# First batch of a fused attention, MLP and expert kernel: another order of its head pairs, 128-wide transposes for two of them, and two units moved to a later place

## The chip, the cores and the metric

One core of one Trainium2 chip runs the whole program. The time is device microseconds (us) of one execution. The kernel before has a median of 770.23 us over three runs (769.16 to 770.8).

## What is computed

Three layers follow each other: masked attention over 4 batches and 8 heads, a gelu-like MLP over the 2304 rows that the attention gives, and an expert layer in which each row may go to one of 8 experts. Heads 0 to 3 use a local mask, heads 4 to 7 a strided one.

```python
    # attention: q, k, v are (4, 8, 576, 64)
    scores = scale * np.matmul(q, k.transpose(0, 1, 3, 2))
    mask_local = (rel >= 0) & (rel < stride)                    # stride = 32
    mask_strided = (rel >= 0) & (pos[None, :] % stride == pos[:, None] % stride)
    attn = np.exp(scores - max); attn = attn / (sum + 1e-09)
    return np.matmul(attn, v)
    # MLP: x is (2304, 512), w_in (512, 2048), w_out (2048, 512)
    h = x @ w_in
    g = h * (1.0 / (1.0 + np.exp(-1.702 * h)))
    return g @ w_out
    # experts: rows with x @ w_skip > 0 get x + gate * (relu(x @ w1[e]) @ w2[e]), e = argmax of x @ w_gate
```

## The kernel before

The 8 heads are worked on as four pairs, called hp: hp 0 and 1 are local, hp 2 and 3 strided. A pair is first loaded (`load_qk`), then transposed by TensorE into `qT` and `kb` (`emit_T`, with the copies out of PSUM in `t_evac`), then worked through in three units of up to two windows each (u = 0, 1, 2). A unit has three parts: S1 multiplies q by k into `sc`, adds the mask (VectorE, "pt,st<-sc,mloc" or "mstr"), takes the exponential (ScalarE) and normalises (GpSimd); S2 transposes the probabilities (`tp`, `pT`); S3 multiplies by V (`pv`) and writes the result as a high and a low part into `xT`, the input of the MLP. The rows of the strided V are first permuted through a DRAM buffer `vp_d` by transfers of GpSimd's queue (`permute_v`), and then loaded into `vstr`.

The MLP runs in 9 groups of 256 rows with 16 steps each. Step m of a group is `emit_A` (12 matmuls into `h` with the weights wi[m], then ScalarE's tanh and VectorE's product "g<-g,h") and, two steps later, `emit_B` (6 matmuls into `acc` with wo[m]). The weights come as fp32 and are split into a high and a low part before use, 32 tiles of 128x1024 in all. One such conversion (`conv_w`, "conversion" below) is three VectorE operations through a PSUM tile (L169, L170, L171), one ScalarE copy (L175) and one GpSimd subtraction (L176). Step m needs 2m conversions. The first group of the MLP is written behind batch 0's attention, and batch 1's attention runs between the first group's steps.

Each engine takes its instructions in one fixed order. The kernel writes its pieces in program order (`attn_pieces(0)`, from piece CV0 on a conversion after every third one, then the steps), and a scheduler that models the engines' times may move instructions of different engines and pieces against each other. SP issues nearly all loads, in order as well: an issue that has to wait holds up those behind it. Batch 0's order of pairs is 0, 2, 1, 3. The numbers in names such as raw_114 or p_165 tell buffers apart.

Of the kernel before, what the change touches and what calls it, by code (L numbers as in the profile page):

```python
# [31 lines left out]
FBT = 1  # L32
# [16 lines left out]
AS, AE = 3, 2  # L49
CV0, CV1 = 16, 3  # L50
WN = [0, 0, 2, 4]
PM, PC = 10, 15
# [6 lines left out]
AS1 = 9  # L59
KD = (0, 2)  # L60


@with_exitstack
def attn_moe_moe_kernel(ctx: ExitStack, tc: tile.TileContext, q, k, v, w_in, w_out, w_skip, w_gate, w1, w2, out):
# [11 lines left out]
    def big_tile(dt, name):  # L76
        return big.tile([128, 1024], dt, tag="big", name=name)
# [144 lines left out]
    with ExitStack() as ph1:  # L222
# [37 lines left out]
        def order(b):  # L260
            return [(b, 0), (b, 2), (b, 1), (b, 3)]

        def load_qk(b, hp):
            h0 = 2 * hp
            first = False
            if b == 0:
                raw = big_tile(F32, "raw0").rearrange("p (i h j d) -> p i h j d", i=2, j=4, h=2)
                if "tails" not in raws:
                    t = big_tile(F32, "tails")
                    raws["tails"] = t[:, 0 : H * D].rearrange("p (h d) -> p h d", h=H)  # L270
                    lst0.append(t[:, H * D : H * D + 256])
                    first = True
                rawt = raws["tails"][:, h0 : h0 + 2, :]
            else:
                raw = ap_.tile([128, 2, 4, 2, D], F32, tag="raw", bufs=2, name="raw")
                rawt = ap_.tile([128, 2, D], F32, tag="rawt", bufs=2, name="rawt")
            raws[b, hp] = raw, rawt
            for i, src in enumerate((q, k)):
                for h in range(2):
                    nc.sync.dma_start(out=raw[:, i, :, h, :] if b else raw[:, i, h, :, :], in_=src[b, h0 + h, 0:512, :].rearrange("(p j) d -> p j d", j=4))  # L280
                if b > 0:
                    nc.sync.dma_start(out=rawt[64 * i : 64 * i + 64], in_=src[b, h0 : h0 + 2, 512:576, :].rearrange("h p d -> p h d"))
            if first:
                for i, src in enumerate((q, k)):
                    nc.sync.dma_start(out=raws["tails"][64 * i : 64 * i + 64], in_=src[b, :, 512:576, :].rearrange("h p d -> p h d"))
# [38 lines left out]
        def t_evac(b, hp, jobs):  # L324
# [4 lines left out]
            for which, j, p in jobs:  # L329
                for lo, hi in ((0, 128),) if which == 0 else ((0, 64), (64, 128)):  # L330
                    d = [t_views(hp, qt[y] if which == 0 else kt[y][lo:hi, lo // 64], j) for y in ((z,) if b <= FB else (0, 1))]
                    ops.append((t_source(hp, p[lo:hi], j), d))
                    if b == 0 and hp in KD and which == 1:
                        nc.vector.tensor_copy(d[0], ops[-1][0])
# [12 lines left out]
        def emit_T(b, hp, which):  # L347
# [6 lines left out]
            for j in range(4):  # L354
                if b:
                    nc.tensor.transpose(out=p1[:, j, :], in_=raw[:, which, j].rearrange("p h d -> p (h d)"), identity=ident)  # L356
# [13 lines left out]
        def geom(hp, u, j):  # L370
# [8 lines left out]
            return w * RG * NTS, n, w * RG * NTS, n, mstr[0:n, 0:n]  # L379

        def ntile(hp, u):
            return 1 if hp >= 2 and u == 2 else 2

        def emit_S1(b, hp, u):
            nj = ntile(hp, u)
            sc = ps.tile([128, 2, 2, 128], F32, tag="sc" if b else ("sc", "acc0", "acc0")[u], name="sc")
            qn0 = geom(hp, u, 0)[1]
            for j in range(nj):
                q0, qn, k0, kn, _ = geom(hp, u, j)
                qt, kt = qk_bufs["q"], qk_bufs["k"]  # L390
                z = order(0).index((0, hp)) % 2
                prods = ((z, z),) if b <= FB else ((0, 0), (0, 1), (1, 0))
# [54 lines left out]
        def emit_S3(b, hp, u):  # L447
            pT = ust.pop((b, hp, u))
            nj = ntile(hp, u)
            qn = geom(hp, u, 0)[1]  # L450
            pv = ps.tile([128, 2 * 126], F32, tag="pv" if b else "acc1", name="pv")
            for j in range(nj):
# [49 lines left out]
        def attn_pieces(b):  # L502

            pairs = order(b)
            units = [(bb, hp, u) for bb, hp in pairs for u in range(3)]
            res = []
# [10 lines left out]
            for n in range(len(units) + 2):  # L517
                if n < len(units):
                    bb, hp, u = units[n]
                    if u == 0 and (b > FBT or n == 0):  # L520
                        res += T(n // 3)
                    res.append(lambda a=units[n]: emit_S1(*a))
                    if u == (TU1 if b else TU) and b <= FBT and n // 3 < 3:
                        res += T(n // 3 + 1)
                if 1 <= n <= len(units):
                    res.append(lambda a=units[n - 1]: emit_S2(*a))
                if n >= 2:
                    res.append(lambda a=units[n - 2]: emit_S3(*a))
                if n % 3 == 1 and n < len(units):
                    nx = pairs[n // 3 + 1] if n // 3 + 1 < 4 else order(b + 1)[0] if b + 1 < B else None  # L530
                    if nx and nx not in vt and (b or nx[0] == 0):
                        res.append(lambda a=nx: load_v(*a))
            return res


# [246 lines left out]
        nw = 0  # L782
        for n_, a in enumerate(order(0)):
            load_next_qk()
            if n_ == 0:
                permute_v(0, nc.gpsimd)
            load_v(*a)
            nw += WN[n_]
            loads_to(nw)
        for n_, p in enumerate(attn_pieces(0)):  # L790
# [4 lines left out]
        rq = []  # L795
        att = []
        nB = 0
        for s_ in range(NG * NM + LAG8):
            gi, m = divmod(s_, NM)
            if gi < NG:  # L800
# [22 lines left out]
                emit_A(gi, m)  # L823
            left_slots = 2 * (32 - (AE if s_ >= 32 else AE1) - s_ % 32)
            if att and s_ < NM:

# [265 lines left out]
```

## Time and profile before

| | |
|---|---|
| median of three runs | 770.23 us (769.16 to 770.8) |
| the profiled execution: its time, its span | 770.98 us, 769.3 us |
| TensorE matmul busy | 727.2 us (95% of the span) |
| VectorE, ScalarE, GpSimd busy | 357.1, 339.2, 164.0 us |
| TensorE's granted clock, 40 slices, tenths | 9985899999999999999999999999999899999998 |

The span is what lies between the first and the last instruction; some 1.7 us of the profiled execution's time lie around it. The profiled execution is 0.75 us above the median. Granted clock 1.00 is 2.4 GHz, 0.50 is 1.2 GHz. A slice of the last row is 19.2 us. In the rows further down, a busy time is that of an engine's instructions; "[idle before <-X]" is how long the engine had nothing to do ahead of a row and what released it.

### The profile page before, as it was taken

How to read it: one execution, taken by the hardware profiler on the slowest of the kernel's cores; microseconds unless marked ns; L12 is line 12 of the kernel's file. 1: busy time of each engine (PE TensorE's matmuls, PEld its weight loads, DVE VectorE, ACT ScalarE, POOL GpSimd, SP SyncE). 2: the span in 40 equal slices, each digit the busy share in tenths (PEclk: the TensorE clock that was granted, in tenths of full speed). 3: DMA queues.
4: the chain of work that ended last, by engine and by line, in shares of the span. 5: the costliest groups of instructions: out<-in, count | busy, mean ns of one | idle time of the engine just before them, and what ended most of it. 6: DMA issues, size and time to landing. Idle time of an engine off the chain costs nothing.

```text
span 769.3 us, 14169 instructions
## 1 busy us (share of the span) xinstructions
PE 727.2 (95%) x4977; PEld 636.6 (83%) x4977; DVE 357.1 (46%) x1452; ACT 339.2 (44%) x1096; POOL 164.0 (21%) x226
## 2 busy tenths in 40 slices
PE   7867999999999999999999999999999699999993
PEld 3545898788788888888888878988998699999993
DVE  2589886545456546355565534353452111121111
ACT  2695677565466566356665533342442111111110
POOL 4265665223013011202210202002021100000001
PEclk9985899999999999999999999999999899999998
DMA  8989811320302222221110010100683499981001
GB/s 244 354 282 258 269 32 34 80 47 11 103 5 66 61 53 39 68 59 22 43 46 1 10 37 15 33 25 14 195 153 99 127 395 397 353 261 41 16 13 33
DMA packets 95984, 84.44 MB, mean 110 GB/s; under 512 B 59412, under 2 KB 74964, under 8 KB 95904
## 3 DMA queue, kind: packets, MB, share of 16 engines
q1 hardware_dynamic: 92608, 78.39, 34.4%
q0 software_dynamic: 3296, 5.05, 2.0%
q8 instruction: 41, 0.67, 0.5%
q14 instruction: 39, 0.32, 0.3%
HBM read 71.00 MB, written 17.68 MB: 115 GB/s over the span
## 4 chain that ended last, share of the span: by engine, by line
PE 71%; issue 13%; DMA 10%; ACT 2%; DVE 2%; SPq 1%; POOL 0%; POOLq 0%; DVEq 0%; ACTq 0%
PE h L548 27%; PE acc L575 27%; DMA wx<-in_moe_w_dram 6%; PE sc L394 4%; PE pv L456 3%; PE tp L437 2%; PE p L360 2%; DMA out_dram<-res,xr 2%; PE p L356 1%; DMA raw<-in_q_dram 1%; PE tr L605 1%; PE p L359 1%; PE lc L619 1%; DMA tab_d<-rows,ix 1%; ACT kb L336 1%
## 5 line engine op out<-in xcount | busy, mean ns | idle before, releaser
L548 PE MATMUL h<-xT,wsp 128*128 128x256 f32 x1728 | 249.7, 289 | 1.3 <-ACT xT L472 1.3
L548 PEld LDWEIGHTS h<-xT,wsp 128*128 128x128 f32 x1728 | 232.1, 192 | 16.6 <-ACT xT L472 2.4
L575 PE MATMUL acc<-wsp,ghl 128*128 128x512 f32 x816 | 226.9, 403 | 0.5 <-ACT wsp L175 0.5
L575 PEld LDWEIGHTS acc<-wsp,ghl 128*128 128x128 f32 x816 | 141.3, 188 | 25.6 <-issue 2.0
L422 POOL TENSOR_TENSOR pt<-pt,st 96x256 f32<-96x256 f32 (+3 forms) x88 | 50.3, 589 | 258.3 <-DVE st L419 106.2
L552 DVE SCALAR_TENSOR_TENSOR g<-g,h 128x256 f32<-128x256 f32 x144 | 60.2, 419 | 92.6 <-ACT g L551 88.6
L551 ACT ACTIVATE g<-h 128x256 f32<-128x256 f32 x144 | 54.8, 382 | 101.6 <-PE h L548 91.9
L564 ACT ACTIVATE ghl<-g 128x256 fp32r<-128x256 f32 (+1 forms) x144 | 57.9, 404 | 59.5 <-DVE g L552 55.4
L932 PE MATMUL h<-xs,wx 128*128 128x160 f32 x512 | 77.7, 306 | 0.0
L412 ACT ACTIVATE pt<-pt,st 96x128 f32<-96x128 f32 (+3 forms) x176 | 67.3, 385 | 16.4 <-DVE st L404 16.0
L932 PEld LDWEIGHTS h<-xs,wx 128*128 128x128 f32 x512 | 73.0, 195 | 0.0
L933 ACT ACTIVATE hT<-h 128x160 f32<-128x160 f32 x64 | 19.4, 303 | 121.3 <-PE h L932 115.2
L941 PE MATMUL h<-hT,wx 128*128 128x160 f32 x512 | 72.4, 299 | 0.0
L565 DVE TENSOR_TENSOR ghl<-g,ghl 128x256 fp32r<-128x256 f32 (+1 forms) x128 | 53.6, 419 | 37.2 <-ACT ghl L564 29.5
L941 PEld LDWEIGHTS h<-hT,wx 128*128 128x128 f32 x512 | 70.3, 190 | 0.0
L394 PE MATMUL sc<-kb,qT 128*96 128x256 f32 (+3 forms) x220 | 45.6, 331 | 5.3 <-ACT kb L336 2.3
L696 POOL DMA_INDIRECT xs_d<-rows,ix x18 | 18.1, 1005 | 134.5 <-DVE ghl L565 36.9
L176 POOL TENSOR_TENSOR wsp<-wcv,wsp 128x512 fp32r<-128x512 f32 x32 | 41.1, 1284 | 22.2 <-ACT wsp L175 17.5
L956 POOL DMA_INDIRECT out_dram<-res,xr x16 | 14.6, 914 | 146.0 <-DVE res L953 87.1
L944 DVE COPY yT<-h 128x160 f32<-128x160 f32 x32 | 10.4, 325 | 75.7 <-PE h L941 75.7
L336 ACT ACTIVATE kb<-p 64x64 fp32r<-64x64 f32 (+3 forms) x56 | 38.5, 687 | 10.1 <-PE p L356 4.0
L394 PEld LDWEIGHTS sc<-kb,qT 128*96 128x96 f32 (+2 forms) x220 | 31.7, 176 | 11.6 <-issue 2.9
(151 smaller groups left out, 781.4 us busy)
## 6 DMA issues: line engine op xcount, KB each, us to landing
wx<-in_moe_w_dram SPq DMA_DIRECT2D x64, 512.0 KB
wraw<-in_moe_w_in_dram SPq DMA_DIRECT2D x16, 512.0 KB
wraw<-in_moe_w_out_dram SPq DMA_DIRECT2D x16, 512.0 KB
raw<-in_q_dram SPq DMA_DIRECT2D x32, 128.0 KB
raw<-in_k_dram SPq DMA_DIRECT2D x32, 128.0 KB
out_dram<-rows SPq DMA_DIRECT2D x16, 256.0 KB
xs_d<-zinit SPq DMA_DIRECT2D x1, 2570.0 KB
xr<-xs_d SPq DMA_DIRECT2D x16, 160.6 KB
```

The lines of the kernel that those rows point to most:

```text
L336: nc.scalar.activation(out=d[0], in_=ops[-1][0], func=AF.Copy)
L394: nc.tensor.matmul(out=sc[0:qn, j, :, 0:kn], lhsT=qt[a][:, q0 : q0 + qn], rhs=kt[c][:, :, k0 : k0 + kn], start=(n_ == 0), stop=(n_ == len( ...
L412: nc.scalar.activation(out=P[0:qn, j, h, 0:kn], in_=P[0:qn, j, h, 0:kn], func=AF.Exp, scale=-1.0, bias=st[0:qn, 0, i : i + 1], accum_out=s ...
L422: nc.gpsimd.tensor_tensor(out=P[0:qn, j, :, 0:kn], in0=P[0:qn, j, :, 0:kn], in1=st[0:qn, 1, 2 * j : 2 * j + 2, None].to_broadcast([qn, 2, ...
L548: nc.tensor.matmul(out=hp_, lhsT=wi[m][:, a, c, :], rhs=x[z], start=(n_ == 0), stop=(n_ == 3 * NC - 1))
L551: nc.scalar.activation(out=g, in_=hp_, func=AF.Tanh, scale=0.851)
L552: nc.vector.scalar_tensor_tensor(out=g, in0=g, scalar=1.0, in1=hp_, op0=ALU.add, op1=ALU.mult)
L564: nc.scalar.activation(out=t[:, 0], in_=g[:, a:z], func=AF.Copy)
L565: (nc.gpsimd if gi == 0 else nc.vector).tensor_tensor(out=t[:, 1], in0=g[:, a:z], in1=t[:, 0].bitcast(F32), op=ALU.subtract)
L575: nc.tensor.matmul(out=acc[gi, i], lhsT=ghl[i][:, a, :], rhs=wo[m][:, z, :], start=(m == 0 and n_ == 0), stop=(m == NM - 1 and n_ == 2),)
L932: nc.tensor.matmul(out=p, lhsT=wx[e, 0, c][:, 128 * m : 128 * m + 128], rhs=x, start=(c == 0), stop=(c == NC - 1))
L941: nc.tensor.matmul(out=p, lhsT=wx[e, 1, k_ // 2][:, o : o + 128], rhs=hT[e][k_ // 4][:, k_ % 4], start=(k_ == 0), stop=(k_ == NF - 1))
```

## The change

Batch 0's pairs go in the order 2, 3, 0, 1, so that the strided ones come first. Pairs 2 and 3 (those not in HM) are loaded with the two heads of a row beside each other, in pieces of 256 bytes rather than 1 KB, and transposed both heads at once, 128 wide. The third unit of pairs 0 and 1 is taken out of `attn_pieces(0)` and written between the first group's steps (`late_pieces`), with PSUM tiles of other tags. Conversions begin after piece 12 rather than 16 of a list that is now two units shorter. The loads of V and of the first weights are written in another order. KD and the condition behind it say which kb copies VectorE does in place of ScalarE: all of pairs 0 and 2 before, the lower half of pair 2 and all of pair 3 now.

```diff
-CV0, CV1 = 16, 3
-WN = [0, 0, 2, 4]
+CV0, CV1 = 12, 3
-KD = (0, 2)
+KD = (2, 3)
+HM = (0, 1)
         def order(b):
-            return [(b, 0), (b, 2), (b, 1), (b, 3)]
+            return [(b, hp) for hp in ((2, 3, 0, 1) if b == 0 else (0, 2, 1, 3))]
...
-                    nc.sync.dma_start(out=raw[:, i, :, h, :] if b else raw[:, i, h, :, :], in_=src[b, h0 + h, 0:512, :].rearrange("(p j) d -> p j d", j=4))
+                    nc.sync.dma_start(out=raw[:, i, h, :, :] if b == 0 and hp in HM else raw[:, i, :, h, :], in_=src[b, h0 + h, 0:512, :].rearrange("(p j) d -> p j d", j=4))
...
-                    if b == 0 and hp in KD and which == 1:
+                    if b == 0 and hp in KD and which == 1 and (lo == 0 or hp == 3):
                         nc.vector.tensor_copy(d[0], ops[-1][0])
...
             for j in range(4):
-                if b:
+                if b or hp not in HM:
                     nc.tensor.transpose(out=p1[:, j, :], in_=raw[:, which, j].rearrange("p h d -> p (h d)"), identity=ident)
...
+        def late_unit(b, hp, u):
+
+            return b == 0 and hp < 2 and u == 2
...
-            sc = ps.tile([128, 2, 2, 128], F32, tag="sc" if b else ("sc", "acc0", "acc0")[u], name="sc")
+            sc = ps.tile([128, 2, 2, 128], F32, tag="sc" if b or late_unit(b, hp, u) else ("sc", "acc0", "acc0")[u], name="sc")
...
-            pv = ps.tile([128, 2 * 126], F32, tag="pv" if b else "acc1", name="pv")
+            if late_unit(b, hp, u):
+                pv = ps.tile([128, 2 * 126], F32, tag="t", bufs=2, name="pv")
+            else:
+                pv = ps.tile([128, 2 * 126], F32, tag="pv" if b else "acc1", name="pv")
...
+        def late_pieces():
+            us = [(0, hp, 2) for hp in (0, 1)]
+            return [lambda f=f, a=a: f(*a) for f in (emit_S1, emit_S2, emit_S3) for a in us]
...
-        for n_, a in enumerate(order(0)):
-            load_next_qk()
-            if n_ == 0:
-                permute_v(0, nc.gpsimd)
-            load_v(*a)
-            nw += WN[n_]
-            loads_to(nw)
+        load_next_qk()
+        permute_v(0, nc.gpsimd)
+        load_next_qk()
+        load_next_qk()
+        load_v(0, 2)
+        load_v(0, 3)
+        loads_to(2)
+        load_next_qk()
+        load_v(0, 0)
+        load_v(0, 1)
+        nw = 4
+        loads_to(nw)
...
+            for _ in range(2):
+                if late_att:
+                    late_att.pop(0)()
```

What this does to TensorE's order shows at the very start of the program. These are its rows at the end of the first pair's transposes, before; p_165 and p_175 are that pair's q and k, each as eight pieces of 64 rows, and p_210 is the second pair's q:

```order
L359 MATMUL p_175<-ident,raw_114 64x128
L360 MATMUL p_175<-ident,raw_114 64x128
L344 MATMUL p_186<-ident,tails 128x128
L394 MATMUL sc<-kb,qT 96x2x96
L394 MATMUL sc<-kb,qT 96x256 x3
L359 MATMUL p_210<-ident,raw_129 64x128
L360 MATMUL p_210<-ident,raw_129 64x128
```

And these are TensorE's first rows now, where p_161 and p_167 are the first pair's q and k, p_198 and p_206 the second's:

```order
L357 MATMUL p_161<-ident,raw_114 128x128 x4
L357 MATMUL p_167<-ident,raw_114 128x128 x4
L345 MATMUL p_174<-ident,tails 128x128
L399 MATMUL sc<-kb,qT 126x2x126 x4
L357 MATMUL p_198<-ident,raw_126 128x128 x4
L357 MATMUL p_206<-ident,raw_126 128x128 x4
L399 MATMUL sc<-kb,qT 72x2x72
L442 MATMUL tp<-ident,pt 126x126 x2
```

Sixteen pieces of a pair have become eight, for the first two pairs; pairs 0 and 1 still have sixteen each.

The second place is VectorE's order around the first product of the MLP ("g<-g,h"). Before, its rows are:

```order
L170 SCALAR_TENSOR_TENSOR cvp<-wraw,cvp 128x512
L171 SCALAR_TENSOR_TENSOR wcv<-wraw,cvp 128x512
L492 TENSOR_TENSOR xT<-pv,xT 128x8x4 x2
L169 TENSOR_SCALAR cvp<-wraw 128x512
L170 SCALAR_TENSOR_TENSOR cvp<-wraw,cvp 128x512
L171 SCALAR_TENSOR_TENSOR wcv<-wraw,cvp 128x512
L169 TENSOR_SCALAR cvp<-wraw 128x512
L552 SCALAR_TENSOR_TENSOR g<-g,h 128x256 x2
L170 SCALAR_TENSOR_TENSOR cvp<-wraw,cvp 128x512
```

Now they are:

```order
L500 TENSOR_TENSOR xT<-pv,xT 128x128
L171 SCALAR_TENSOR_TENSOR wcv<-wraw,cvp 128x512
L500 TENSOR_TENSOR xT<-pv,xT 128x64
L500 TENSOR_TENSOR xT<-pv,xT 128x128
L169 TENSOR_SCALAR cvp<-wraw 128x512
L500 TENSOR_TENSOR xT<-pv,xT 128x128
L170 SCALAR_TENSOR_TENSOR cvp<-wraw,cvp 128x512
L171 SCALAR_TENSOR_TENSOR wcv<-wraw,cvp 128x512
L565 SCALAR_TENSOR_TENSOR g<-g,h 128x256
L169 TENSOR_SCALAR cvp<-wraw 128x512
L170 SCALAR_TENSOR_TENSOR cvp<-wraw,cvp 128x512
L565 SCALAR_TENSOR_TENSOR g<-g,h 128x256
```

Counted from the start of VectorE's order, 15 1/3 conversions stand ahead of the first product before, and 12 now; all of batch 0's attention, the two moved units too, still stands ahead of it.

The third place is TensorE's order where the MLP begins. Before, with v_141 and v_154 the V of pairs 1 and 3, and p_1084 and p_1093 the first transposes of batch 1:

```order
L548 MATMUL h<-xT,wsp 128x256 x2
L437 MATMUL tp<-ident,pt 72x72 x2
L548 MATMUL h<-xT,wsp 128x256 x4
L456 MATMUL pv<-pT,v_141 64x96 x4
L456 MATMUL pv<-pT,v_154 64x126 x4
L356 MATMUL p_1084<-ident,raw 128x128 x4
L456 MATMUL pv<-pT,v_154 64x126 x4
L456 MATMUL pv<-pT,v_154 64x72 x2
L548 MATMUL h<-xT,wsp 128x256 x2
L344 MATMUL p_1089<-ident,rawt 128x128
L356 MATMUL p_1093<-ident,raw 128x128 x4
L548 MATMUL h<-xT,wsp 128x256 x4
```

Now, with vloc and v_153 the V of pairs 0 and 1:

```order
L464 MATMUL pv<-pT,vloc 64x96 x4
L561 MATMUL h<-xT,wsp 128x256 x2
L442 MATMUL tp<-ident,pt 128x96 x4
L561 MATMUL h<-xT,wsp 128x256 x10
L464 MATMUL pv<-pT,v_153 64x96 x4
L464 MATMUL pv<-pT,vloc 64x96 x4
L464 MATMUL pv<-pT,v_153 64x96 x8
L561 MATMUL h<-xT,wsp 128x256 x12
L357 MATMUL p_1068<-ident,raw 128x128 x4
L561 MATMUL h<-xT,wsp 128x256 x12
L588 MATMUL acc<-wsp,ghl 128x512 x4
```

Before, the first two steps' matmuls are strewn among the attention of batch 0; now a step's twelve stand nearly together behind it. The second group begins as the first ends; from shortly ahead of the first run of 15 `acc` matmuls on (it stands between the first two transposes "tr<-ident,rows"), TensorE's order is the same in both kernels to the program's end, apart from line numbers, and so are the orders of the other engines from about there.

## Rows read from the trace of the kernel before

**Rows 1.** Stretches: length, busy us (count) of PE, PEld, DVE, ACT, POOL, clock, DMA, GB/s.

```profile
0.00:32.48 32.48, 26.18 (x113) 14.28 (x113) 10.54 (x57) 12.77 (x39) 11.88 (x36) 1.00 0.96 285
32.48:42.00 9.52, 8.64 (x52) 5.29 (x53) 6.08 (x27) 8.83 (x35) 3.57 (x5) 1.00 1.06 377
42.00:79.78 37.78, 24.12 (x147) 17.95 (x146) 35.31 (x108) 28.27 (x97) 23.60 (x28) 0.64 0.90 256
79.78:122.99 43.21, 43.21 (x272) 38.96 (x271) 38.34 (x96) 29.19 (x83) 32.32 (x35) 0.96 0.41 120
122.99:146.01 23.02, 21.96 (x165) 18.75 (x164) 13.05 (x42) 15.08 (x45) 7.57 (x10) 1.00 0.26 68
```

**Rows 2.** TensorE, the first row of the order that both kernels share.

```profile
146.01 3.75 PE L575 MATMUL acc<-wsp,ghl 128*128 128x512 f32 x15
```

**Rows 3.** The chain of waits, two pieces: start, length, what.

```profile
13.38 3.48 PE sc L394 x8
...
69.14 0.71 DVE cvp L170
```

**Rows 4.** TensorE in order of time: start, length, line, form, count.

```profile
3.05 0.39 PE L359 MATMUL p<-ident,raw 128*64 128x128 f32 x1 [3.05 <-DMA raw<-in_q_dram]
...
11.01 0.48 PE L344 MATMUL p<-ident,tails 128*128 128x128 f32 x1
...
28.03 0.27 PE L359 MATMUL p<-ident,raw 128*64 128x128 f32 x1
...
30.37 1.12 PE L394 MATMUL sc<-kb,qT 128*126 128x252 f32 x4
...
69.60 1.12 PE L356 MATMUL p<-ident,raw 128*128 128x128 f32 x4
```

**Rows 5.** VectorE in order of time.

```profile
11.11 2.61 DVE L334 COPY kb<-p 64x512 f32<-64x512 f32 x4 [11.11 <-PE p L360]
15.32 0.26 DVE L404 CUSTOM_DVE_ANT_0 pt<-sc,mloc 96x96 f32<-96x96 f32 x1 [1.60 <-PE sc L394]
...
32.48 0.69 DVE L169 TENSOR_SCALAR cvp<-wraw 128x512 int32<-128x512 int32 x1
...
79.78 0.75 DVE L552 SCALAR_TENSOR_TENSOR g<-g,h 128x256 f32<-128x256 f32 x2 [1.13 <-ACT g L551]
...
122.99 0.42 DVE L552 SCALAR_TENSOR_TENSOR g<-g,h 128x256 f32<-128x256 f32 x1
```

**Rows 6.** VectorE's groups, 0 to 79.78: line, form, count | busy, mean ns | idle before.

```profile
L169 DVE TENSOR_SCALAR cvp<-wraw 128x512 int32<-128x512 int32 x16 | 11.0, 688 | 0.2
...
L171 DVE SCALAR_TENSOR_TENSOR wcv<-wraw,cvp 128x512 int32<-128x512 int32 x15 | 10.3, 683 | 0.8
...
L334 DVE COPY kb<-p 64x512 f32<-64x512 f32 x4 | 4.3, 1064 | 15.2 <-PE p L360 15.2
```

**Rows 7.** GpSimd in order of time: a V permutation and the strided mask.

```profile
6.37 1.34 POOL L307 DMA_DIRECT2D vp_d<-in_v_dram  x2
...
8.69 0.32 POOL L116 TENSOR_SCALAR_AFFINE_SELECT mstr<-mstr 126x126 f32<-126x126 f32 x1
```

**Rows 8.** Line L171 alone in one stretch: length, busy us (count), clock, DMA, GB/s.

```profile
79.78:122.99 43.21, 9.58 (x14) 0.96 0.41 120
```

**Rows 9.** DMA queue 1, 128 to 136 (pieces of 256 bytes): packets, MB, share.

```profile
q1 hardware_dynamic: 2608, 0.64, 35.4%
```

**Rows 10.** SP's issues in order of time: V of pair 2, first and last weights.

```profile
11.51 0.39 SPq L301 DMA_DIRECT2D vstr<-vp_d  x1
...
12.84 1.29 SPq L156 DMA_DIRECT2D wraw<-in_moe_w_in_dram  x2
...
82.72 0.36 SPq L158 DMA_DIRECT2D wraw<-in_moe_w_out_dram  x1
```

**Rows 11.** TensorE by stretch around 82 us: length, busy (count), granted clock, DMA, GB/s.

```profile
80.00:82.00 2.00, 2.00 (x9) 0.50 0.99 306
...
84.00:86.00 2.00, 2.00 (x15) 1.00 0.90 262
```

More of the change, by code (lines that the diff above doesn't have):

```diff
@@ L266, in load_qk @@
             if b == 0:
-                raw = big_tile(F32, "raw0").rearrange("p (i h j d) -> p i h j d", i=2, j=4, h=2)
+                raw = big_tile(F32, "raw0")
+                raw = raw.rearrange("p (i h j d) -> p i h j d", i=2, j=4, h=2) if hp in HM else raw.rearrange("p (i j h d) -> p i j h d", i=2, j=4, h=2)
                 if "tails" not in raws:
@@ L390, in emit_S1 @@
                 qt, kt = qk_bufs["q"], qk_bufs["k"]
-                z = order(0).index((0, hp)) % 2
+                z = order(b).index((b, hp)) % 2
                 prods = ((z, z),) if b <= FB else ((0, 0), (0, 1), (1, 0))
@@ L504, in attn_pieces @@
             pairs = order(b)
-            units = [(bb, hp, u) for bb, hp in pairs for u in range(3)]
+            units = [(bb, hp, u) for bb, hp in pairs for u in range(3) if not late_unit(bb, hp, u)]
             res = []
@@ L519, in attn_pieces @@
                     bb, hp, u = units[n]
+                    pi = pairs.index((bb, hp))
                     if u == 0 and (b > FBT or n == 0):
-                        res += T(n // 3)
+                        res += T(pi)
                     res.append(lambda a=units[n]: emit_S1(*a))
-                    if u == (TU1 if b else TU) and b <= FBT and n // 3 < 3:
-                        res += T(n // 3 + 1)
+                    if u == (TU1 if b else TU) and b <= FBT and pi < 3:
+                        res += T(pi + 1)
                 if 1 <= n <= len(units):
@@ L528, in attn_pieces @@
                     res.append(lambda a=units[n - 2]: emit_S3(*a))
-                if n % 3 == 1 and n < len(units):
+                if b and n % 3 == 1 and n < len(units):
                     nx = pairs[n // 3 + 1] if n // 3 + 1 < 4 else order(b + 1)[0] if b + 1 < B else None
-                    if nx and nx not in vt and (b or nx[0] == 0):
+                    if nx and nx not in vt:
                         res.append(lambda a=nx: load_v(*a))
             return res
+        def late_pieces():
+            us = [(0, hp, 2) for hp in (0, 1)]
+            return [lambda f=f, a=a: f(*a) for f in (emit_S1, emit_S2, emit_S3) for a in us]
         gl = {}
@@ L796, in attn_moe_moe_kernel @@
         att = []
+        late_att = late_pieces()
         nB = 0
```

## Prediction

> **What bounds the kernel now.** I read the stages first [rows 1]. The change touches the program only up to 146.01 us: from there on both kernels run the same instructions in the same order [rows 2], and what is left is TensorE's MLP steps and the experts, one behind the other. The experts' weights are loaded into the tiles that the MLP gives back, so they move with it. I therefore take the whole effect as the shift of the moment at which that run of 15 matmuls begins.
>
> The stages show three regimes. Up to 32.48 us no engine but TensorE is full: VectorE works 10.5 of 32.5 us. From 42 to 79.78 VectorE works 35.3 of 37.8 us (0.935) while TensorE works 24.1, at 1.2 GHz for most of it (0.64 on average). From 79.78 to 122.99 TensorE works all of 43.2 us and VectorE 38.3: both are nearly full. The chain of waits says the same: it starts with transposes and S1 on TensorE, and around 70 us runs over the conversions on VectorE [rows 3]. TensorE in order of time [rows 4] shows what the start is made of: sixteen 64-row pieces of the first pair from 3.05 to 11.01 us, 7.96 us. VectorE in order of time [rows 5] gives the marks: first copy at 11.11, first mask at 15.32, first conversion at 32.48, first two products of the MLP at 79.78, the fifteenth at 122.99.
>
> So the amount of VectorE's work up to the fifteenth product, and how early it can be packed densely, sets the time. The change does not remove conversions; it removes idle time ahead of them.
>
> **The sum.** One conversion costs VectorE three operations of 0.69 us, 2.06 together [rows 6].
>
> *Start to first conversion.* The first two pairs need eight 128-wide transposes each instead of sixteen pieces. Four such took 1.12 us at 1.2 GHz (from the stretch around 70 us) [rows 4], so a pair takes 2.24 instead of 7.96. Both heads must have landed now; I give that 0.8 us, so they end near 6.1. Behind them stand one kb copy of 1.06 us on VectorE [rows 6], the other half at the same time on ScalarE, and S1, whose first result can be masked near 8.3. But the strided mask is written by GpSimd only at 8.69 + 0.32 = 9.01 [rows 7], behind its permutations of V, which do not move. So the first mask comes at 9.05 instead of 15.32: 6.3 us earlier. The second pair saves some 3 more, and the third pair, still sixteen pieces, gives them back if the clock has not risen by then: 7.96 us at 1.2 GHz against 2 x 2.34 at 2.4 GHz (28.03 to 30.37 is half of a pair). First conversion: 32.48 - 6.3 = 26, with 23 and 29 as bounds (everything at the high clock; 3 us of waits for loads).
>
> *First conversion to first product.* Before, VectorE worked 6.08 + 35.31 = 41.4 us here, of which 15 1/3 conversions are 31.6 and the rest 9.8. Now 12 conversions stand there, 24.7 us, and the rest less two masks that moved ahead, 9.4: 34.1 us. At the density of 0.935 that is 36.5; the first ten microseconds before were thinner (3.4 us idle), for which I add 2.5. First product at 26 + 36.5 + 2.5 = 65 us, against 79.78. ScalarE, which gets one kb copy more (some 1.3 us), worked 28.3 of 37.8 us in this stretch and has the room.
>
> *First to fifteenth product.* This is where part of the gain is given back: 17 conversions stand here now instead of 14 1/3 (14 for L171 [rows 8]). The rest of VectorE's 38.3 us was 8.8; with four masks more and their small operations I take 10.1, so 35.0 + 10.1 = 45.1 us. At 0.935 that is 48.2 us, at the 0.887 that this stretch had before (then paced by TensorE) 50.8. I take 50: fifteenth product at 115 against 122.99. TensorE needs some 43 to 44 us for the same steps and would wait 6 in all; the bound moves from TensorE to VectorE there.
>
> *To the shared order.* 23.0 us before. At the fifteenth product TensorE has nine transposes, two S1 matmuls and eight probability transposes fewer left than before, together some 2.5 us; I count 1, since VectorE and ScalarE pace the end of the group as well. The run of 15 begins at 115 + 22 = 137 instead of 146: 9 us earlier.
>
> Against the profiled execution that is 770.98 - 9.0 = 762.0 us; against the median, which is 0.75 lower, **761.2 us**.
>
> *What is costed at nothing.* The 1 MB of pairs 2 and 3 now comes in pieces of 256 bytes. In such pieces 0.64 MB took 35.4% of 8 us, 2.83 us of all engines [rows 9], against 377 GB/s in the weights' stretch [rows 1]: 1 MB costs 4.4 instead of 2.7 us, so the weights behind land up to 1.7 us later. Up to 16 further tiles are ordered ahead of the one being converted, which covers that; uncovered it would be 1.7 us at the first conversion, inside the bound of 29. The Trainium skill, "DMA: Bandwidth & Descriptors", section Specifications, asks for at least 512 bytes a piece for full rate, and thus speaks against this edit; the row agrees in direction, with 226 GB/s. By it the forecast would be at most that 1.7 us later. On SP the V load of batch 1 and two stores of `left_d` now wait for the moved units, with the last six weight loads behind them: they go out near 68 us instead of up to 82.72 [rows 10], and the first of these weights is not converted until past 100, so 30 us cover it. The moved units themselves are the same work; they stay ahead of the first product, so their "late" place gains nothing by itself.
>
> **The rivals.**
> *TensorE stays the bound of the first group.* If VectorE packs better than 0.935, the run of 15 comes 66.2 us (79.78 to 146.01) behind the first product, plus about 1 us for batch 1's nine transposes and 2.9 for a step of twelve at the low clock that was already done by 79.78 before. From 64 us that gives 134: 12 us gained, 758 us. For it: VectorE's idle time there before was mostly short waits for ScalarE. Against it: 45 us of work do not fit into 43.
> *V of the strided pairs comes late.* The first `pv` now stands between the third pair's transposes, and needs V that went through `vp_d`. GpSimd issues the last permutations at 6.37 to 7.71 and SP issued the load at 11.51 [rows 7, 10], with four engines' other loads still queued; `pv` wants it near 21. Each microsecond that it lands later delays everything behind it on TensorE; at 26 the time is 766, at 30 the gain is gone. For it: DMA is full there (0.96 over the stretch). Against it: 9 us lie between issue and need.
> *No change.* VectorE's order is fixed by a scheduler's estimate; if its waits fill the stretch to 79 us again (density 0.7 between 26 and 75), all of the early start is lost: 770 us.
> *Slower: the low clock.* TensorE ran at 1.2 GHz from 80 to 82 us, where it already worked without a gap, and at 2.4 from 84 to 86 [rows 11]. Now it has less to do in the first 60 us, and between 65 and 115 it waits some 12% of the time. If the clock stays low through that stretch, 43 us of work become over 80, and the run of 15 begins near 167: 791 us. It decides from about 30 us of low clock beyond the first product: half of that is lost, 6 us of it in TensorE's new slack and 9 against the gain. Against it: at the low clock TensorE has no waits for the first six steps, for which 12 conversions lie ready, so it is gapless, as it was when the clock rose before. The skill's "TensorE: Matmul & The Clock Gate", Part 4, says that transposes do not count as work for the clock; by it the first two pairs, now transposes alone, would leave the clock low longer. No row here tells that apart, since half of the pieces before were plain matmuls. I had already counted the third pair at the low clock, so by that rule the time would be up to 3 us later, with the fourth pair.
>
> **Chances.** The forecast's case (757 to 766 us) 0.60; TensorE-bound 0.14; V late or other waits that leave some gain (766 to 768.7) 0.08; no change (within 0.2% of the median, 768.7 to 771.8, about what a measurement here can tell) 0.10; slower 0.08. Faster by over 0.2%: 0.82 by these; I give 0.80, with 0.11 and 0.09. The range, 756 to 769.5 us, takes in the TensorE-bound case and the late V; the likeliest case alone spans 757 to 766.
>
> **What would show it.** First mask near 9.1 us, first conversion at 23 to 29, first product near 65 with 12 conversions ahead of it; between there and the fifteenth product VectorE busy over 0.9 and TensorE with waits for conversions; the run of 15 near 137. Wrong: a first conversion past 30 (loads or V), a first product past 72 (packing), a clock of 0.50 past 85 us, or the stretch after 146 not moving along.

## The result and the profile after

The changed kernel takes 759.13 us (median of four runs, 758.55 to 759.86) against 769.76 us for the kernel before beside it (four runs, 769.16 to 770.8): a ratio of 0.9861 with the interval 0.9844 to 0.9878, 10.6 us less. The forecast was 761.2 us. The profiled execution took 758.55 us. These lines of its page answer to the small table of before (busy time, share of the span, count; then the granted clock in 40 slices):

```profile
span 756.8 us, 14113 instructions
...
PE 715.0 (94%) x4945; PEld 630.5 (83%) x4945; DVE 352.9 (47%) x1450; ACT 340.1 (45%) x1098; POOL 164.2 (22%) x226
...
PEclk9968999999999999999999999999999899999998
```

The stages, cut at the changed kernel's own marks (first conversion, first product, fifteenth product, the run of 15), answer to [rows 1]; the columns are the same:

```profile
0.00:27.07 27.07, 17.13 (x80) 11.75 (x81) 9.27 (x51) 15.32 (x44) 11.16 (x35) 1.00 0.94 229
27.07:65.45 38.38, 30.17 (x193) 21.74 (x192) 34.07 (x126) 29.97 (x119) 24.00 (x31) 0.73 1.03 326
65.45:115.39 49.94, 46.92 (x295) 40.77 (x295) 43.89 (x117) 40.34 (x107) 36.37 (x39) 1.00 0.68 191
115.39:135.33 19.94, 19.23 (x148) 16.36 (x146) 12.49 (x32) 9.92 (x29) 7.66 (x8) 1.00 0.17 47
135.33:756.80 621.47, 601.55 (x4236) 539.86 (x4234) 253.14 (x1128) 244.58 (x803) 85.02 (x113) 0.99 0.30 89
```

The run of 15 begins at 135.33 instead of 146.01 [rows 2], 10.7 us earlier, and the median fell by 10.6: what follows moved along. VectorE's marks in order of time answer to [rows 5]:

```profile
7.65 1.06 DVE L335 COPY kb<-p 64x512 f32<-64x512 f32 x1 [7.65 <-PE p L357]
...
13.09 0.29 DVE L409 CUSTOM_DVE_ANT_0 pt<-sc,mstr 126x126 f32<-126x126 f32 x1 [2.64 <-PE sc L399]
...
27.07 0.69 DVE L169 TENSOR_SCALAR cvp<-wraw 128x512 int32<-128x512 int32 x1
...
65.45 0.41 DVE L565 SCALAR_TENSOR_TENSOR g<-g,h 128x256 f32<-128x256 f32 x1
...
115.39 0.39 DVE L565 SCALAR_TENSOR_TENSOR g<-g,h 128x256 f32<-128x256 f32 x1
```

The first mask is 4 us later than forecast, and yet the first conversion is within about 1 us of the forecast, the first and the fifteenth product within half of one. TensorE in order of time shows both halves of that; its first rows answer to [rows 4]:

```profile
4.69 1.09 PE L357 MATMUL p<-ident,raw 128*128 128x128 f32 x4 [4.69 <-DMA raw<-in_q_dram]
6.53 1.09 PE L357 MATMUL p<-ident,raw 128*128 128x128 f32 x4 [0.75 <-DMA raw<-in_k_dram]
...
10.91 3.69 PE L399 MATMUL sc<-kb,qT 128*126 128x252 f32 x8 [2.72 <-ACT kb L337]
14.39 1.75 PE L357 MATMUL p<-ident,raw 128*128 128x128 f32 x8
...
18.47 0.27 PE L360 MATMUL p<-ident,raw 128*64 128x128 f32 x1 [0.52 <-PE tp L442]
18.67 0.43 PE L361 MATMUL p<-ident,raw 128*64 128x128 f32 x2
...
23.14 0.65 PE L464 MATMUL pv<-pT,vstr 126*64 126x126 f32 x8
...
64.68 0.60 PE L357 MATMUL p<-ident,raw 128*128 128x128 f32 x4
```

Two things can be seen here. The first S1 waits until 10.91 for a kb copy of ScalarE, 3.3 us after the k transposes end (6.53 + 1.09 = 7.62). And the third pair's pieces, from 18.47 on, take 0.27 us, half a pair in some 2.3 us. TensorE's speed had doubled before that, within the second pair's eight transposes at 14.39: they took 1.75 us, where four took 1.09 at 4.69 and 0.60 at 64.68, which puts the change near 15.8 us. The kernel before runs pieces of its second pair at that time, and they become fast near 18.3 us, inside the row at 17.98:

```profile
16.65 0.42 PE L359 MATMUL p<-ident,raw 128*64 128x128 f32 x1
17.00 0.69 PE L360 MATMUL p<-ident,raw 128*64 128x128 f32 x2
...
17.98 0.56 PE L360 MATMUL p<-ident,raw 128*64 128x128 f32 x2
18.47 0.30 PE L359 MATMUL p<-ident,raw 128*64 128x128 f32 x1
18.70 0.43 PE L360 MATMUL p<-ident,raw 128*64 128x128 f32 x2
```

ScalarE of the changed kernel, in order of time, names the wait ahead of S1:

```profile
8.75 1.08 ACT L337 ACTIVATE kb<-p 64x512 f32<-64x512 f32 x1 [1.84 <-DVE kb L335]
9.86 0.29 ACT L337 ACTIVATE qT<-p 128x64 f32<-128x64 f32 x1
10.48 0.28 ACT L337 ACTIVATE kb<-p 64x64 f32<-64x64 f32 x1 [0.34 <-DVE kb L335]
```

Its half of kb begins only when VectorE's half has ended (7.65 + 1.06 = 8.71); the two halves were not copied at the same time.

What the earlier start is worth can be counted on VectorE, up to the start of the third operation of the 32nd and last conversion: 138.2 us before, 127.4 after. The second and third stretch of before, from the first conversion to the first product and from there to the last conversion:

```profile
32.48:79.78 47.30, 32.76 (x197) 23.24 (x198) 41.39 (x134) 37.09 (x131) 27.18 (x33) 0.71 0.93 281
79.78:138.20 58.42, 57.90 (x382) 51.97 (x381) 46.88 (x123) 39.80 (x112) 38.61 (x43) 0.97 0.35 100
```

and the third of after:

```profile
65.45:127.40 61.95, 58.41 (x383) 50.91 (x384) 52.27 (x134) 45.78 (x121) 42.75 (x46) 1.00 0.55 155
```

Each stretch's length less its VectorE work is VectorE's idle time: 21.9, 5.9 and 11.5 us before (the first from [rows 1]), 17.8, 4.3 and 9.7 after. Of the 10.8 us by which the last conversion moved, 7.6 are idle time (4.1, 1.6 and 1.9 by stretch) and 3.2 are work that no longer stands ahead of it (98.8 against 95.6 us). By this count the gain is spread over all three stretches, and the head gives less than half.

The same can be counted on TensorE, up to the run of 15. Before and after, in one stretch each:

```profile
0.00:146.01 146.01, 124.11 (x745) 95.22 (x745) 103.33 (x324) 94.13 (x295) 78.94 (x113) 0.89 0.68 200
0.00:135.33 135.33, 113.45 (x713) 90.61 (x713) 99.71 (x322) 95.54 (x297) 79.20 (x113) 0.92 0.75 216
```

TensorE is idle for 21.9 us in both. By this count all of the 10.7 us are time in which TensorE was busy before and no longer is: 32 matmul rows fewer, and a smaller part of the rest at the low clock (mean 0.92 against 0.89). Each count is bookkeeping, true by itself; neither shows which engine's time is the cause. The edits below do more.

### The profile page after: what moved, and what is told of

It reads as the page before. It is cut to its first block, busy times and chain, and to the rows that moved or that the text cites. A ratio compares the mean times of both kernels' runs of the same rounds, so it can differ in the third digit from the quotient of the medians.

```text
span 756.8 us, 14113 instructions
## 1 busy us (share of the span) xinstructions
PE 715.0 (94%) x4945; PEld 630.5 (83%) x4945; DVE 352.9 (47%) x1450; ACT 340.1 (45%) x1098; POOL 164.2 (22%) x226
## 4 chain that ended last, share of the span: by engine, by line
PE 67%; issue 15%; DMA 8%; ACT 5%; DVE 2%; SPq 1%; POOL 0%; POOLq 0%; ACTq 0%; DVEq 0%
PE h L561 26%; PE acc L588 26%; DMA wx<-in_moe_w_dram 4%; PE sc L399 4%; PE pv L464 3%; PE tp L442 2%; DMA out_dram<-res,xr 2%; ACT pt L417 2%; ACT kb L337 1%; PE p L357 1%; PE tr L618 1%; DMA tab_d<-rows,ix 1%; PE lc L632 1%; PE p L361 1%; SPq L929 0%
## 5 line engine op out<-in xcount | busy, mean ns | idle before, releaser
L561 PE MATMUL h<-xT,wsp 128*128 128x256 f32 x1728 | 245.8, 287 | 2.5 <-POOL wsp L176 0.7
L561 PEld LDWEIGHTS h<-xT,wsp 128*128 128x128 f32 x1728 | 229.3, 191 | 18.3 <-issue 2.1
L978 POOL DMA_INDIRECT out_dram<-res,xr x16 | 14.6, 914 | 145.5 <-DVE res L975 103.0
L337 ACT ACTIVATE kb<-p 64x64 fp32r<-64x64 f32 (+3 forms) x58 | 39.7, 684 | 10.7 <-DVE qT L340 3.8
```

The source lines that it names most:

```text
L337: nc.scalar.activation(out=d[0], in_=ops[-1][0], func=AF.Copy)
L561: nc.tensor.matmul(out=hp_, lhsT=wi[m][:, a, c, :], rhs=x[z], start=(n_ == 0), stop=(n_ == 3 * NC - 1))
```

## The experiments

All took part in comparisons with the kernel before on the same chip (its median there 768.93, 769.54 and 769.98 us). The table holds the marks of each profile in us; "idle" is VectorE's up to the 32nd conversion, worked out as above; the experts' first matmul (h<-xs,wx) is a late mark which every kernel has. Each row is explained below.

| kernel | first mask | first conversion | first product | 32nd conversion | idle | experts | median |
|---|---|---|---|---|---|---|---|
| before | 15.32 | 32.48 | 79.78 | 138.2 | 39.4 | 597.62 | 769.76 |
| after | 13.09 | 27.07 | 65.45 | 127.4 | 31.8 | 585.69 | 759.13 |
| after, again | 13.01 | 26.74 | 65.08 | 127.6 | 31.9 | 587.07 | 759.54 |
| all pairs in 64-row pieces | 19.32 | 30.63 | 79.88 | 136.6 | 39.3 | 595.06 | 767.81 |
| all pairs 128 wide | 12.77 | 25.50 | 62.65 | 130.4 | 33.7 | 590.04 | 761.17 |
| before, two pairs wide | 11.62 | 29.45 | 67.24 | 131.2 | 33.3 | 588.45 | 758.76 |
| units unmoved | 12.77 | 26.32 | 67.02 | 124.2 | 28.0 | 583.76 | 755.00 |
| units unmoved, again | 12.84 | 26.49 | 67.22 | 124.4 | 28.5 | 584.37 | 757.75 |
| units unmoved, CV0 = 16 | 12.85 | 26.99 | 67.53 | 124.5 | 28.6 | 582.81 | 755.62 |
| units unmoved, all wide | 12.70 | 25.15 | 64.78 | 129.7 | 29.9 | 586.98 | 758.27 |
| after, TensorE work added | 13.36 | 27.33 | 66.52 | 130.7 | 34.3 | 588.87 | 760.58 |
| before, TensorE work added | 15.21 | 32.43 | 78.31 | 141.1 | 41.8 | 600.30 | 771.85 |
| after, shorter conversions | 12.74 | 26.56 | 69.27 | 123.7 | 46.1 | 583.25 | 755.25 |

**All pairs in 64-row pieces.** The changed kernel with only the wide transposes undone.

```diff
-HM = (0, 1)
+HM = (0, 1, 2, 3)
```

> The changed kernel with all four pairs of batch 0 loaded in 1 KB pieces and transposed in sixteen 64-row pieces again; order of pairs and moved units stay. My theory (VectorE's idle time ahead of the conversions is what was saved, and the narrow transposes made it): first conversion near 33 us instead of 27, fifteenth product some 5 us later, 764 us (761 to 767). Rival (order of pairs and moved units make the gain): 759 to 760.

Measured: 767.81 us (766.54 to 771.49, 12 runs), ratio 0.999 (0.9969 to 1.0011). Nearly all of the gain is gone with this one edit, 8.3 to 8.7 us of it (767.81 less 759.54 and 759.13), where I had expected 764 and at most 767. Its stretches:

```profile
0.00:30.63 30.63, 23.93 (x82) 12.16 (x82) 8.22 (x40) 10.87 (x30) 11.12 (x35) 0.94 0.96 267
30.63:79.88 49.25, 35.08 (x228) 24.34 (x227) 41.43 (x143) 37.01 (x136) 26.56 (x33) 0.79 0.88 275
79.88:136.60 56.72, 55.80 (x376) 50.14 (x377) 47.68 (x127) 42.78 (x118) 40.03 (x44) 1.00 0.42 117
```

VectorE's idle times are 22.4, 7.8 and 9.0 us: against the changed kernel 4.6 more in the head, 3.5 more in the second stretch, 0.6 less in the third. The first two pairs' slow pieces delay the first mask to 19.32, and the second stretch is not denser for it. On TensorE it is idle for 22.0 of the 144.74 us up to the run of 15 and busy for 122.7, so the lost gain is TensorE's busy time here too (9.3 us more than after), at the same mean clock of 0.92.

**Before, with two pairs wide.** The other way round: the kernel before with this edit alone, on the two pairs that it has first (0 and 2); order of pairs, units, conversions and loads as before.

```diff
+HM = (1, 3)
-                if b:
+                if b or hp not in HM:
```

(and the same lines of `load_qk` as in the change)

> The kernel before with nothing but the first two pairs of its own order (0 and 2) loaded and transposed 128 wide. My theory: most of the gain comes with this alone: 762 us (759 to 765). Rival (the order of pairs is needed, the strided pairs first): 767 to 770.

Measured: 758.76 us (757.97 to 759.98), ratio 0.9865 (0.9838 to 0.9891). The edit alone, with the smaller load pieces and the order that the scheduler makes of it, gives what the whole change gives. Its first conversion is only 3.0 us earlier than before, its first product 12.5:

```profile
0.00:29.45 29.45, 20.45 (x96) 12.91 (x97) 11.07 (x57) 14.34 (x45) 11.92 (x36) 0.94 0.96 255
29.45:67.24 37.79, 27.45 (x174) 18.82 (x172) 32.79 (x120) 29.48 (x116) 22.92 (x30) 0.78 1.01 330
67.24:131.20 63.96, 61.82 (x398) 54.32 (x398) 54.02 (x137) 44.93 (x121) 43.30 (x47) 0.97 0.48 131
```

Much of that is order: 11 conversions stand ahead of the first product here, not 15 1/3, and what was put off is paid behind it (63.96 us to the last conversion against 58.42). The first product is therefore a poor mark; the last conversion moved by 7.0 us, the run of 15 by 7.9 (138.12), the experts by 9.2. TensorE's idle time up to the run of 15 is 22.1 us, as before.

**Units unmoved.** The changed kernel with the third units of pairs 0 and 1 left in batch 0's list, and with the PSUM tiles that they have there.

```diff
-            return b == 0 and hp < 2 and u == 2
+            return False
...
-            us = [(0, hp, 2) for hp in (0, 1)]
+            us = []
```

> The changed kernel with the third units of pairs 0 and 1 back among batch 0's pieces. My theory (they stay ahead of the first product anyway, the same VectorE work): 759 us, within 1.5 of the changed kernel. Rival (moving them is part of the gain): 762 or more.

Measured: 755.0 us (754.13 to 759.57, 6 runs), ratio 0.9837 (0.9803 to 0.9871): neither; its median lies 4 us under the change's, though the intervals of the two ratios overlap. The runs lay in two clusters, so I repeated it beside the changed kernel on one chip.

> The changed kernel unaltered, as a yardstick beside the same kernel with its two units unmoved, on one chip. If moving the two units costs some 4 us by itself, as the two earlier measurements on different chips suggest, this stands at 759 (758 to 760) and the other 4 us lower. If that difference was a difference between chips or between executions, the two stand within 1.5 us of each other.

> The changed kernel with its two units left in the attention's list, once more. Theory: moved units cost time, because behind the first product VectorE stood 6.0 us ahead of products that waited for TensorE and ScalarE with them moved and 1.6 us without: 755 (754 to 757), at least 2 us under the changed kernel of this call. Rival: the four executions near 754.5 and two near 759.3 of the first time are two ways in which the same program goes, and the difference is not the units': 757 to 760.

Measured: 759.54 us (758.85 to 760.78) with the units moved, ratio 0.987 (0.9846 to 0.9893), and 757.75 (754.08 to 759.62, 6 runs) unmoved, ratio 0.983 (0.9801 to 0.986). By the medians that is 1.8 us, the intervals overlap, and 757.75 lies in the rival's range and not in the theory's. The profiles say more: the two unmoved ones reach the 32nd conversion at 124.2 and 124.4 against 127.4 and 127.6, and the experts' first matmul at 583.76 and 584.37 against 585.69 and 587.07. The profiled execution of 757.65 us in the second set had lost its difference behind that mark, in instructions that all kernels share (171.5 us from there to the end of the span against 169.1 in the first). So moving the units costs about 3 us up to the last conversion and 1.3 to 3.3 at the experts, and the rest was the tail's own spread.

Where the 3 us stand is shown by the groups of VectorE's instructions between first product and last conversion: the product's line, its busy time, and behind the second bar how long VectorE stood idle ahead of it. Before:

```profile
L552 DVE SCALAR_TENSOR_TENSOR g<-g,h 128x256 f32<-128x256 f32 x19 | 7.9, 418 | 7.9 <-ACT g L551 7.8
```

After:

```profile
L565 DVE SCALAR_TENSOR_TENSOR g<-g,h 128x256 f32<-128x256 f32 x19 | 7.8, 412 | 6.0 <-ACT g L564 5.9
```

Units unmoved:

```profile
L565 DVE SCALAR_TENSOR_TENSOR g<-g,h 128x256 f32<-128x256 f32 x19 | 7.9, 415 | 1.6 <-ACT g L564 1.5
```

A product that comes up in VectorE's fixed order before TensorE and ScalarE have made its g holds up the conversions behind it: 4.4 us more with the units moved (6.6 against 1.5 us in the repetition). This goes with the loss in this pair of kernels, but it is not shown to be its cause: nothing was changed in these stalls alone, and with all four pairs wide (below) it is the other way round, 3.8 us with the units moved and 6.7 without, though the unmoved kernel is the faster one there as well.

**Conversions from piece 16 again**, units unmoved.

```diff
-CV0, CV1 = 12, 3
+CV0, CV1 = 16, 3
```

> The changed kernel with its units unmoved and conversions begun from piece 16 again, so that beside the kernel before only the order of the pairs, the wide transposes of two of them, the kb copies and the order of loads differ. If the place from which conversions are written matters little (a scheduler moves them anyway; 46 of VectorE's 1445 rows change): the same as with 12, 755.5 to 757.8. If it is what lets VectorE begin early: 2 to 4 us more, 758.5 to 761.

Measured: 755.62 us (755.45 to 756.07), ratio 0.9814 (0.9788 to 0.984). With the units unmoved CV0 does not matter, as the first case said. With the other two unmoved ones this is the best version of the study, and faster than both kernels: 3.9 us under the changed kernel's 759.54, measured in another comparison, whose ratio was 0.987. Against the kernel before it has only the order of pairs, the two wide pairs, KD and the order of loads. Beside the kernel before with two wide pairs (758.76), order, KD and loads together are worth some 3 us by the medians, though the intervals of the ratios just touch; which of the three, no run tells.

**All pairs 128 wide**, with the units moved and unmoved.

```diff
-HM = (0, 1)
+HM = ()
```

> The changed kernel with all four pairs transposed 128 wide. My theory: the third and fourth pair's pieces fall by half, 3.8 us of TensorE each, and part of VectorE's idle time between 19 and 45 us goes with them: first product near 61, 756 us (753 to 758). Rival (from the first conversion on only VectorE's total counts, and that does not change): 758 to 760.

> All four pairs transposed 128 wide and the two units unmoved. Theory: an earlier first conversion (25.5 with four wide pairs, 26.3 with two) is worth less than what the order of instructions loses behind the first product, so this stands where two wide pairs with unmoved units stand, or above: 756 to 760. Rival (the head sets the time, and only the moved units spoilt the earlier run with four wide pairs): 1 to 3 us lower than with two, 753 to 755.5.

Measured: 761.17 us (759.23 to 762.78), ratio 0.9899 (0.987 to 0.9927) with the units moved; 758.27 (757.32 to 759.38), ratio 0.9845 (0.9819 to 0.9872) unmoved. The first lies above both cases, the second where the theory put it. Both have the earliest first conversions (25.50, 25.15) and neither is better than with two wide pairs; the moved units cost 2.9 us by the medians here as well. The first one's stretches show where it goes:

```profile
0.00:25.50 25.50, 14.90 (x71) 10.80 (x72) 9.96 (x57) 15.77 (x47) 11.94 (x37) 1.00 0.98 213
25.50:62.65 37.15, 27.89 (x167) 19.49 (x165) 31.47 (x117) 28.63 (x114) 21.98 (x29) 0.68 1.01 329
62.65:130.40 67.75, 60.48 (x387) 52.23 (x386) 55.30 (x137) 46.43 (x122) 43.85 (x47) 0.97 0.56 158
```

VectorE's idle time in the head is down to 15.5 us and in the last stretch up to 12.5: the early start is given back behind the first product. TensorE waits longer as well, 27 us up to the run of 15 in both of these kernels.

**Which engine is the bound behind the first product.** Four more matmuls at the head of each of the first 14 steps of the first group; the next matmul overwrites them, so the result is unchanged. Once on the changed kernel, once on the one before.

```diff
             n_ = 0
+            if gi == 0 and m < 14:
+                for _ in range(4):
+                    nc.tensor.matmul(out=hp_, lhsT=wi[m][:, 0, CO[0], :], rhs=xT_get(gi, CO[0])[0], start=True, stop=True)
```

> The changed kernel with four further matmuls into h at the head of each of the first 14 steps of the first group, overwritten by the next one with start=True, so that the result is unchanged: 56 matmuls of 0.12 us, 6.7 us of TensorE at 2.4 GHz. My prediction's step (VectorE has become the bound between the first and the fifteenth product, TensorE waits some 6 us there): most of it hides in TensorE's waits, plus 1 to 2.5 us, 760 to 761.5. Rival (TensorE is still the bound there): plus 5 to 6.7 us, 764 to 766.

> The kernel before with the same 56 further matmuls as the changed kernel had in the experiment that lengthened it by 1.0 us. If TensorE is the bound of the first group before the change, as its 43.2 busy us in 43.2 say, nearly all 6.7 us appear: 773.5 to 776. If VectorE's conversions and the order of its instructions paced the group there as well, plus 0 to 2.5 us: 769 to 772.

Measured: 760.58 us (759.91 to 761.48) on the changed kernel, 1.0 over the 759.54 of the same chip; 771.85 (770.72 to 775.41, 12 runs) on the one before, ratio 1.0032 (1.0012 to 1.0052), 1.9 over its 769.98. The first is as expected. The second is not: 6.7 us of added TensorE work appear as 1.9 (by the interval 0.9 to 4.0) in the kernel whose TensorE I had read as the bound. Its stretch from the first product to the last conversion:

```profile
78.30:141.10 62.80, 62.73 (x433) 57.04 (x433) 49.08 (x129) 43.16 (x117) 39.83 (x43) 0.99 0.39 106
```

Inside this stretch the added matmuls are not hidden. TensorE runs without a gap, and a step of 18 matmuls takes 2.84 us before (89.89 to 92.73), and 3.30 us (85.90 to 89.20) with four more, 0.12 us for each. Before:

```profile
89.89 1.58 PE L575 MATMUL acc<-wsp,ghl 128*128 128x512 f32 x6
91.31 1.59 PE L548 MATMUL h<-xT,wsp 128*128 128x256 f32 x12
92.73 1.09 PE L575 MATMUL acc<-wsp,ghl 128*128 128x512 f32 x4
```

With the work added (L547):

```profile
85.90 0.63 PE L547 MATMUL h<-xT,wsp 128*128 128x256 f32 x4
86.37 1.59 PE L551 MATMUL h<-xT,wsp 128*128 128x256 f32 x12
87.80 1.56 PE L578 MATMUL acc<-wsp,ghl 128*128 128x512 f32 x6
89.20 0.63 PE L547 MATMUL h<-xT,wsp 128*128 128x256 f32 x4
```

What made up for them lies elsewhere. The scheduler planned anew: 13 conversions and part of a 14th stand ahead of the first product, not 15 1/3, and it comes 1.5 us earlier. And the low clock ended earlier; the kernel before reads 0.50 from 80 to 82 [rows 11], this one

```profile
80.00:82.00 2.00, 2.00 (x16) 1.00 0.74 232
```

On the changed kernel, too, the low clock ended earlier (1.00 from 62 to 64 us, where it was 0.59), and TensorE's idle time in the third stretch fell from 3.5 us (3.1 in the repetition) to 1.6. At the first transposes "tr<-ident,rows" both kernels are later by about half of what was added: 147.91 against 144.53, and 136.98 against 133.84 and 134.01. So the runs do not show that TensorE was not the bound of the first group before, and on the changed kernel they show up to 2 us of 6.7 going into TensorE's waits; the rest of the small price came with the clock and the order.

**Shorter conversions.** The changed kernel without the second VectorE operation of each conversion, which leaves out a part of the split of the weights; VectorE has 32 x 0.69 = 22 us less to do.

```diff
-        nc.vector.scalar_tensor_tensor(out=t, in0=r[:, :, 0], scalar=29, in1=t, op0=ALU.logical_shift_right, op1=ALU.bitwise_or)
```

> The changed kernel with each conversion made without its second VectorE operation, which leaves out a part of the split of a weight into a high and a low part: 32 operations of 0.69 us, 22 us less work on VectorE. If VectorE is the bound after the first product as predicted, the 15th product comes some 10 us earlier until TensorE limits it: 753 (750 to 757). If TensorE is the bound there, only the stretch ahead of the first product gets shorter, and the time stays at 757 to 759.

Measured: 755.25 us (754.46 to 757.51), ratio 0.9817 (0.9792 to 0.9842), 4.3 us less, and the fifteenth product 5.4 us earlier (110.0 against 115.4 us), not 10. Its last stretch:

```profile
69.30:123.70 54.40, 53.96 (x365) 48.55 (x366) 33.49 (x103) 38.69 (x111) 35.57 (x40) 1.00 0.47 141
```

VectorE is idle for 20.9 of the 54.4 us, TensorE for 0.4, and a fifth of what VectorE saved reached the time: here VectorE's conversions are no longer the bound. The order changed as well (17 conversions stand ahead of the first product, which comes at 69.27, later than the 65.45 with whole conversions). Behind the first product 22 us of VectorE's work and 6.7 of TensorE's each moved the time by a part of their size; neither engine sets it alone.

## Why the prediction was right, and where its steps were not

*Right by its marks.* First conversion 26 forecast, 27.07 measured; first product 65 with 12 conversions ahead, 65.45 with 12; VectorE's work in that stretch 34.1, 34.07; fifteenth product 115, 115.39; the rest moved along with its mark (621.47 us with 4236 matmuls against 623.29 with the same 4236, and the granted clock at 0.50 from 204 to 206 us only in the kernel before).

*The 2.1 us between 761.2 and 759.13* are mostly one mis-sized term. Of the 2.5 us of transposes, S1 and probability transposes that TensorE no longer has behind the fifteenth product I counted 1; the stretch shrank from 23.02 [rows 1] to 19.94, by 3.1 us, and the run of 15 came 1.7 us earlier than 137. The other 0.5 us is the median of the kernel before, 769.76 beside the changed one and 770.23 when I forecast.

*The head held two errors that cancelled.* I let the strided mask, ready at 9.01 [rows 7], limit the first mask. Measured 13.09: k landed at 6.39 and its transposes ended at 7.62, not 6.1; the two kb copies came one behind the other, with three small copies of the last rows behind them (9.86 to 10.76); and the first unit's S1, four rows of the trace, took 2.0 us. Against that I took the third pair at the low speed, 7.96 us, and it ran at 0.2 to 0.3 us a piece, since TensorE was fast from about 15.8 us on (in the kernel before from about 18.3); I had read only that kernel's pieces at 3.05 and 28.03 [rows 4], not those between. That the first conversion came within 1.1 us of the 26 is luck in this part. The Trainium skill, "TensorE: Matmul & The Clock Gate", Part 4, says that transposes do not count as work for the clock in the same way; by it the two wide pairs alone would have left the third slow. Here the speed doubled near 15.8, but S1 matmuls had run from 10.91 to 14.6 as well, so the run neither bears the rule out nor contradicts it.

*The 256-byte pieces* were costed at up to 1.7 us and hidden. In the head the DMA engines were 0.94 busy at 229 GB/s, against 0.96 at 285 [rows 1]; with all four pairs in such pieces 0.98 at 213, with none (the same loads in 1 KB pieces) 0.96 at 267. The Trainium skill, "DMA: Bandwidth & Descriptors", section Specifications, asks for at least 512 bytes a piece for full rate: these four agree in direction, though the heads differ in length and in what they load. The price of the pieces alone was not measured; whatever it is, the 10 us that the two wide pairs give are counted with it.

*"The late place gains nothing by itself"* failed: it costs about 3 us. I had looked at where the moved units stand, and they do stand ahead of the first product; I had not looked at what the planner does with the products behind it.

*"The bound moves from TensorE to VectorE"* is not shown. TensorE busy 43.2 of 43.2 us [rows 1] is no proof that it alone was the bound before, and the added matmuls do not refute it either: they appear in full inside the stretch and are made up for by an earlier product and an earlier end of the low clock. After the change TensorE waited 3.0 us between the first and the fifteenth product, not 6, and VectorE's share was 0.88, not the 0.9 that I had named as a sign: both engines are nearly full there. The forecast of the stretch (50 us, measured 49.94) held because I had taken its length between the two readings, with VectorE's work at 45.1 us (measured 43.89). That the change removes idle time ahead of the conversions is one of two accounts: 7.6 us of VectorE's idle time went, and on TensorE's count none did, but 10.7 us of busy time.

*Of the rivals,* V of the strided pairs was in time: the first `pv` at 23.14 waits for nothing. The low clock ended as the products began; by stretches of 2 us, clock after the count:

```profile
60.00:62.00 2.00, 1.69 (x18) 0.50 1.07 244
62.00:64.00 2.00, 2.00 (x15) 0.59 0.99 313
64.00:66.00 2.00, 1.36 (x13) 1.00 0.98 268
```

The TensorE-bound rival's 758 us lies nearer to the result than the forecast does, and its stretch from the first product to the run of 15, 66.2 + 1 + 2.9 = 70.1 us, was measured at 69.88. TensorE waits 3.7 us in that stretch, against 1.1 before, so it does not fit in full; but no run here excludes it.

*What the change consists of,* in the end: by the medians, the wide transposes of two pairs, with their loads and the order made of them, give some 10 us by themselves; pair order, kb copies and loads give about 3 more; the moved units take 2 to 4 back; the earlier conversions do nothing with the units unmoved. That the wide transposes make the gain is shown both ways, by taking them out and by adding them alone; by which engine it reaches the end is open.

## What to carry to other kernels

When two engines hand work to each other in fixed orders, neither busy share names the bound. Adding up an engine's idle time to a mark that every kernel has, stretch by stretch, says what changed, but do it for both engines: here VectorE's idle time fell by 7.6 us, and TensorE's did not fall at all. A test that adds work to one engine has to be read with the clock and the new order as well, since both moved when it was added. Measure the parts of a composite edit alone: here one part gave about as much as the whole, and another took away what a third had added. A mark in the middle, such as the first product, moves when a scheduler puts work off, and proves nothing until the work put off is counted too.

## What the runs showed of the hardware that I had not expected

Before and after, the granted clock reads 1.00 over the whole head, yet four 128-wide transposes took 1.09 us at 4.69 and 0.60 at 64.68, where it also reads 1.00; 1.12 is what they took at 69.60 in the kernel before [rows 4], where it reads 0.50. At the start of this program the duration of an instruction tells the speed, the granted clock does not. The moment at which the speed doubled differs from kernel to kernel: near 18.3 us before, near 15.8 after, near 13.4 in the kernel before with two pairs wide (four transposes at 12.96 took 0.84 us) and near 19 with all pairs in 64-row pieces. In each of the four it came after the first S1 matmuls had begun (13.38, 10.91, 9.68 and 17.11 us); the pieces that ran without a gap from 3.05 to 11.01 in the kernel before had not raised it.

TensorE's matmuls of the MLP run without a gap and at an even price at granted 1.00: 2.84 us for a step of 18, 3.30 with four more.

The same instructions behind the experts' first matmul took 169.1 to 171.7 us to the end of the span in thirteen profiles (752.9 less 583.76 with the units unmoved, 769.3 less 597.62 before). Differences under 2 us between two kernels are better read from a mark ahead of that stage than from single times.
